# Reordering the first key/value groups of a fused linear-attention and gated-MLP kernel

## The chip, the core and the metric

The kernel runs on one core of a Trainium2 chip. The metric is device time in microseconds. Times come from several executions of each kernel (e5, e6, e9 and e10: one each); "before" is always run again on the same chip, and in the same rounds where there were several. Each profile is of one execution; its clock starts at the first instruction, so it ends about 1.7 us below the timed figure of that execution. The engines are named as in the profile: PE (matmul), PEld (weight load), DVE (vector), ACT (scalar), POOL, and SP, whose queue issues transfers.

## The reference, cut to what matters

```python
x = A_x                                         # 2048 tokens x 1024
h = x + linear_attention(layernorm(x), wqkv, wo)   # pk = phi(k); kv = sum_s pk^T v
h2 = h + reglu_mlp(layernorm(h), W_gate, W_up, W_down)
# phi(t) = (t + 1 if t > 0 else exp(t)) + 1e-6
```

The change touches only the start: layer norm of the first tokens, and the K and V projections.

## The kernel before

Tokens come in 16 blocks of 128. K and V are projected for two blocks at a time with a Strassen-like scheme: seven products P1 to P7 in place of eight, on sums of weight quarters (`w_sums`) and sums of token tiles (`x_sums`), both made on DVE. The groups run in the order k0, v2, k1, v3, k2, and so on: `k_group(p)` handles blocks 2p and 2p+1, `v_group(p)` runs two pairs ahead, and the first four blocks get their V directly (`v_piece`). Inside a group PE works through P1, P7, P6, P2, P5, P4, P3, and ACT copies partial results between PSUM banks, so that two later products can accumulate on the same start ("fork copies", fk1 after P1 and fk2 after P6):

```python
prod(a, X(0, 0), W(0, 0), True, "P1")
ident_act(bank(b), bank(a), ..., name + "fk1")     # P6 accumulates on this copy
hook(1)
prod(f, SX(2), TW(2), True, "P7")
ident_act(s7, bank(f), ...)
hook(2)
prod(b, SX(1), TW(1), False, "P6")
ident_act(bank(c), bank(b), ..., name + "fk2")     # P5 accumulates on this copy
hook(3)
prod(a, X(1, 0), W(1, 0), False, "P2")
...                                             # exp of this product
hook(4)
prod(c, SX(0), TW(0), False, "P5")
ident_act(sc, bank(c), ...)                     # P3 waits for this read
s22[0]()                                        # DVE add
hook(5)
prod(b, X(1, 1), TW(3), False, "P4");  s21[0]() # DVE add
hook(6)
...                                             # exp of the first sum
prod(c, SX(3), W(1, 1), False, "P3")
...                                             # exp of the second plain product (s12)
pend[1] = list(s22[2:]) + s12 + list(s21[1:])   # finished in the next group's hook(1)
```

A `hook` is where other work is put into the engines' queues: statistics of later blocks (on ACT, as squares in halves q0 and q1, or on DVE), norms and the transposes of the normalised blocks by DMA, and `kvacc`, 64 small matmuls for a pair of blocks that add pk^T v into one bank.

```python
def T1d(st):                                    # transpose by DMA, then the next load into that slot
    dma_t(sl_tx[k], xnT[:, :, st * P:(st + 1) * P], xn[:, k, :], ...)
    if st + NX1 < NST:
        load_x1(st + NX1)
```

Of the kernel before, what the change touches and what calls it, by code (L numbers as in the profile page):

```python
# [132 lines left out]
def bass_sequential_preLN__linear_attn_block__glu_gated_reglu__prompt_kernel(  # L133
# [28 lines left out]
    NST = S // P  # L162
# [5 lines left out]
    KH = NDC // 2  # L168
# [36 lines left out]
    with es:  # L205
# [44 lines left out]
        TWv = RW[:].bitcast(f16).rearrange("p (j k c) -> p j k c", j=4, k=KH)  # L250
# [156 lines left out]
        B_TWv = bufs("TWv_", 4)  # L407
# [484 lines left out]
        def ln1_stats_act(st, split=False):  # L892
            i = st % NX1
            k = len(ln1_a) % 3
            ln1_a[st] = k
            return act_stats(x1[:, i, :], B_x1[i], xn[:, st % NXN, :], B_xn[st % NXN], s1[:, k, :], B_s1[k],
                             "ln1_%d" % st, split)
# [60 lines left out]
                b = banks[i % len(banks)]  # L958
                mm(bank(b, 512), zeros_t[:, 0:P], zeros_t, True, True, [B_zeros], B_bank[b], "dummy")

        def v_piece(st, h, mid=()):
            b = alloc_bank(P1_POOL)
            nt = ND2 + h
            mid = dict(mid)
            for dc in range(NDC):
                if dc in mid:
                    mid[dc]()
                if st < 2:
                    xa, bx = xcT[:, st, dc, :], B_xcT[st][dc // HDC]
                else:  # L970
                    xa, bx = xnT[:, dc, st * P:(st + 1) * P], xnT_buf(st, dc)
                mm(bank(b, NW), xa, wkv[:, dc, nt * NW:(nt + 1) * NW],
                   dc == 0, dc == NDC - 1, [bx, B_wkv[nt][0 if dc < WKH else 1]], B_bank[b],
                   "v_%d_%d" % (st, h))
            v_copy(b, st, h)

        v_k = {}

# [7 lines left out]
        def v_copy(b, st, j):  # L986
            sc, rd = (1.0, []) if st >= 2 else (rstd[:, v_k[st], :], [B_rstd[v_k[st]]])
            PL.add("act", lambda e: e.activation(out=v_out(st, j), in_=gw(bank(b)), func=ACTF.Identity, scale=sc),
                   reads=[B_bank[b]] + rd, writes=[B_v[st % NV][j]], name="v_%d_%d" % (st, j))
# [45 lines left out]
        def sgroup(pool, tok_major, X, SX, W, TW, e11, e12, e21, e22, name, hooks=(), isphi=True, last=False):  # L1035

            hooks = dict(hooks)

            def prod(b, x, w, start, nm):
                (xf, xr), (wf, wr) = x, w  # L1040
                for kk in range(KH):
                    xa, wa = xf(kk), wf(kk)
                    l, r = (xa, wa) if tok_major else (wa, xa)
                    o = bank(b)
                    if len(r.shape) == 3:
                        o = o.rearrange("p (a b) -> p a b", b=r.shape[2])
                    mm(o, l, r, start and kk == 0, kk == KH - 1, xr + wr, B_bank[b], name + nm, skip=True)

            def hook(i):
                for f_ in pend.pop(i, ()):  # L1050
                    f_()
                if i in hooks:
                    hooks[i]()

            a = alloc_bank(pool)
            f = alloc_bank(pool)
            b = alloc_bank(pool, True)
            prod(a, X(0, 0), W(0, 0), True, "P1")
            ident_act(bank(b), bank(a), [B_bank[a]], [B_bank[b]], name + "fk1")
            hook(1)  # L1060
            prod(f, SX(2), TW(2), True, "P7")
            grp[0] += 1
            s7, b7 = [(atmp, B_at), (btmp[:, 1, :], B_bt[1])][grp[0] % 2]
            sc, bc = btmp[:, 0, :], B_bt[0]
            ident_act(s7, bank(f), [B_bank[f]], [b7], name + "s7")
            hook(2)
            c = alloc_bank(pool, True)
            prod(b, SX(1), TW(1), False, "P6")
            ident_act(bank(c), bank(b), [B_bank[b]], [B_bank[c]], name + "fk2")
            hook(3)  # L1070
            prod(a, X(1, 0), W(1, 0), False, "P2")
            for f_ in e11(bank(a), B_bank[a]):
                f_()
            hook(4)
            prod(c, SX(0), TW(0), False, "P5")
            ident_act(sc, bank(c), [B_bank[c]], [bc], name + "sc")
            s22 = e22(bank(f), B_bank[f], sc, bc)
            s22[0]()
            hook(5)
            prod(b, X(1, 1), TW(3), False, "P4")  # L1080
            s21 = e21(bank(b), B_bank[b], s7, b7)
            s21[0]()
            hook(6)
            for f_ in s22[1:2]:
                f_()
            prod(c, SX(3), W(1, 1), False, "P3")
            s12 = list(e12(bank(c), B_bank[c]))
            if isphi:
                s12.pop(0)()
            if last:  # L1090
                pend[1] = s12 + [s21[1]]
                return [s22[2], s21[2]]
            pend[1] = list(s22[2:]) + s12 + list(s21[1:])
            hook(7)

        pend = {}
# [42 lines left out]
        wv_ = wkv[:, :, D:2 * D]  # L1139
# [1004 lines left out]
            f_()  # L2144
        twk = w_sums(wkv, bw_k, tw_k, B_TWk, "TWk", KH)
        twv = w_sums(wv_, bw_v, tw_v, B_TWv, "TWv", KH)
        twq = w_sums(wq, bw_q, TWq, B_TWq, "TWq", KH // 2)

        v_piece(0, 0, {5: lambda: T1c(1, 0), 7: lambda: T1c(1, 1)})
# [13 lines left out]
        v_piece(2, 1, {4: lambda: T1(3), 6: m5})  # L2163
        q5()
        x_sums(0)
        twk.pop(0)()
        ln1_norm(4)
        T1d(4)
        m6, q6a, q6b = ln1_stats_act(6, True)
# [5 lines left out]
        twk.pop(0)()  # L2175
        twv.pop(0)()
        twv.pop(0)()
        v_piece(3, 1)
        for i in range(2):
            load_wq(i)  # L2180
        NP_ = NST // 2

        def kv_hooks(p, nq):

            sq = []
            A, B = 2 * p + 6, 2 * p + 7

            def k1():
                if p > 0 and A < NST:
                    ln1_stats(A)  # L2190
                for _ in range(nq[0]):
                    twq.pop(0)()

            def k4():
                if p == 0:
                    x_sums(2, 0)

            def k5():
                if p == 0:
                    x_sums(2, 1)  # L2200
                elif p + 2 < NP_:
                    x_sums(p + 2, 0)
                if p == 0:
                    m_, q0_, q_ = ln1_stats_act(B, True)
                    m_()
                    sq.extend([q0_, q_])
                while p > 0 and late_q:
                    late_q.pop(0)()

            def k6():  # L2210
                if p == 0:
                    twv.pop(0)()
                elif p + 2 < NP_:
                    x_sums(p + 2, 1)
            return {1: k1, 4: k4, 5: k5, 6: k6}, sq

        def norm(st):
            if st < NST:
                ln1_norm(st)
                T1d(st)  # L2220
# [5 lines left out]
        def kvaccs(p):  # L2226
            kvacc(2 * p)
            kvacc(2 * p + 1)

        late_q = []  # L2230
        NQ = {2: (0, 1), 3: (0, 1), 4: (0, 1), 5: (2, 2), 6: (1, 0)}
        for p in range(NP_):
            nq = NQ.get(p, (0, 0))
            hooks, sq = kv_hooks(p, nq)
            if p == 0:
                hooks[1], hooks[3] = q6a, q6b
            if p == NP_ - 1:
                hooks[7] = lambda: kvaccs(NP_ - 2)
            k_group(p, hooks)
            if p + 2 < NP_:  # L2240
                late = []

                def v3(p=p, sq=sq, late=late):
                    if sq:
                        sq.pop(0)()
                    if p == 0:
                        norm(6)
                        x_sums(1)
                    else:
                        norm(2 * p + 6)  # L2250
                        if 2 * p + 9 < NST:
                            m_, q0_, q_ = ln1_stats_act(2 * p + 9, True)
                            q0_()
                            late += [m_, q_]

                def v4(sq=sq):
                    if sq:
                        sq.pop(0)()

                def v5(p=p, late=late):  # L2260
                    norm(2 * p + 7)
                    if p == 0:
                        m_, q0_, q_ = ln1_stats_act(9, True)
                        m_()
                        late_q.extend([q0_, q_])
                    elif late:
                        late[0]()
                        late_q.append(late[1])

                def v6(p=p, nq=nq):  # L2270
                    kvaccs(p)
                    for _ in range(nq[1]):
                        twq.pop(0)()
                v_group(p + 2, {3: v3, 4: v4, 5: v5, 6: v6})
        assert not twq and not twv and not twk
        for i in range(ND2):
            load_wo(i)
# [1 line left out]
        for r in range(2):  # L2279
            for ct in range(NG // 2):  # L2280
                hooks = {}
# [41 lines left out]
        for p_ in range(NPASS):  # L2323
            fill = []
            for q in range(NPAIR):
                if q + 1 < NPAIR and p_ == 0:
                    fill = fill + t_sums((q + 1) * 2)
                mid = [[], [], [], [], []]
# [3 lines left out]
                if p_ == 0:  # L2332
# [4 lines left out]
                    if LQ <= q < LQ + TPP:  # L2337
                        m_, sq_, n_ = late_steps(q - LQ)
# [161 lines left out]
```

## Time and profile before

| | before |
|---|---|
| time, median (lowest to highest) of 4 runs | 719.93 us (719.61 to 719.95) |
| span of the profile | 718.3 us |
| PE / DVE / ACT busy | 99% / 83% / 53% |
| PE wait for the first fork copies of k0 and v2 | 1.6 us, the two of them |

PE is busy nearly all the time, and the profile's rows overlap (one of four matmuls is shown 1.03 us long, but the next starts 0.87 us later), so "busy" hides small gaps; gaps are read from the distance between the starts of products of the same form (0.87 us for four matmuls). The views that carry this are in the prediction.

### The profile page before, as it was taken

How to read it: one execution, taken by the hardware profiler on the slowest of the kernel's cores; microseconds unless marked ns; L12 is line 12 of the kernel's file. 1: busy time of each engine (PE TensorE's matmuls, PEld its weight loads, DVE VectorE, ACT ScalarE, POOL GpSimd, SP SyncE). 2: the span in 40 equal slices, each digit the busy share in tenths (PEclk: the TensorE clock that was granted, in tenths of full speed). 3: DMA queues.
4: the chain of work that ended last, by engine and by line, in shares of the span. 5: the costliest groups of instructions: out<-in, count | busy, mean ns of one | idle time of the engine just before them, and what ended most of it. 6: DMA issues, size and time to landing. Idle time of an engine off the chain costs nothing.

```text
span 718.3 us, 13075 instructions
## 1 busy us (share of the span) xinstructions
PE 711.7 (99%) x4979; PEld 387.4 (54%) x4979; DVE 597.4 (83%) x1009; ACT 383.9 (53%) x679; POOL 110.4 (15%) x178
## 2 busy tenths in 40 slices
PE   8999999999999999999999999999999999999998
PEld 4344444444444444444444568865555555547887
DVE  6988867799776889889888787878888888988885
ACT  4877656764941456686756102036766667643010
POOL 3321100000360103422320002320000000000331
PEclk9999999999999999999999999999999999999999
DMA  9852244014998787999998999995343534267996
GB/s 297 259 106 72 38 122 159 23 31 96 206 203 253 243 267 236 272 322 291 301 275 269 318 259 305 314 252 157 93 132 104 160 98 137 82 199 248 318 323 188
DMA packets 195102, 144.18 MB, mean 201 GB/s; under 512 B 53984, under 2 KB 172512, under 8 KB 195040
## 3 DMA queue, kind: packets, MB, share of 16 engines
q1 hardware_dynamic: 190048, 138.77, 66.2%
q0 software_dynamic: 4032, 3.67, 3.6%
q10 hardware_dynamic: 960, 0.92, 0.4%
q8 instruction: 39, 0.64, 0.4%
q14 instruction: 23, 0.19, 0.1%
HBM read 98.76 MB, written 32.51 MB: 183 GB/s over the span
## 4 chain that ended last, share of the span: by engine, by line
PE 93%; DVE 3%; DMA 2%; issue 1%; SPq 0%; ACT 0%; ACTq 0%
PE ps L777 93%; DMA RE<-in_A_x_dram 1%; DMA RAB<-in_A_wqkv_dram 1%; DVE RW L999 1%; DVE RC L999 1%; SPq L573 0%; DVE RWG L1024 0%; DVE RE L865 0%; DVE RX L1108 0%; DVE RE L1850 0%; DVE RX L862 0%; DVE st L791 0%; DVE RH L1024 0%; DVE RWG L1790 0%; ACT RX L858 0%
## 5 line engine op out<-in xcount | busy, mean ns | idle before, releaser
L782 ACT ACTIVATE ps<-ps 128x512 f32<-128x512 f32 (+1 forms) x233 | 122.3, 531 | 200.5 <-PE ps L777 171.8
L777 PE MATMUL ps<-RC,RO 128*128 128x512 f16 x616 | 143.0, 369 | 0.0
L777 PEld LDWEIGHTS ps<-RC,RO 128*128 128x128 f16 x616 | 60.3, 98 | 57.9
L777 PE MATMUL ps<-RH,RWG 128*128 128x512 bf16 (+1 forms) x396 | 91.2, 365 | 0.0
L777 PE MATMUL ps<-RC,RWG 128*128 128x512 f16 x320 | 79.0, 379 | 0.5 <-ACT ps L782 0.4
L782 ACT ACTIVATE RE<-ps 128x512 f32<-128x512 f32 (+3 forms) x85 | 49.3, 597 | 39.1 <-PE ps L777 28.9
L777 PE MATMUL ps<-RH,RO 128*128 128x512 bf16 (+1 forms) x256 | 63.3, 379 | 0.0
L777 PEld LDWEIGHTS ps<-RH,RWG 128*128 128x128 bf16 x396 | 38.7, 98 | 40.9 <-ACT ps L782 0.2
L1859 POOL DMA_DIRECT2D out_dram<-RX x20 | 18.0, 1282 | 260.9 <-DVE RX L1850 218.7
L777 PE MATMUL ps<-RW,RE 128*128 128x512 bf16 x256 | 57.6, 380 | 0.0
L777 PE MATMUL ps<-RW,RAB 128*128 128x256 f16 (+3 forms) x362 | 52.9, 301 | 0.0
L777 PEld LDWEIGHTS ps<-RC,RWG 128*128 128x128 bf16 (+1 forms) x320 | 30.0, 98 | 37.7 <-ACT ps L782 6.5
L777 PE MATMUL ps<-RAB 128*128 128x512 bf16 (+2 forms) x238 | 49.8, 348 | 0.0
L777 PEld LDWEIGHTS ps<-RW,RAB 128*128 128x128 f16 (+1 forms) x362 | 35.4, 98 | 14.4 <-DVE RX L1850 0.2
L1850 DVE TENSOR_TENSOR RE<-ps,RE 128x512 f32<-128x512 f32 x44 | 30.2, 687 | 15.1 <-PE ps L777 12.4
L1375 DVE TENSOR_TENSOR RO<-RWG 128x1024 f16<-128x1024 bf16 x54 | 36.9, 684 | 4.8 <-DMA RWG<-in_B_W_up_dram 4.8
L777 PEld LDWEIGHTS ps<-RW,RE 128*128 128x128 bf16 x256 | 23.9, 98 | 28.0 <-DVE RXH L1273 0.4
L777 PEld LDWEIGHTS ps<-RH,RO 128*128 128x128 f16 (+1 forms) x256 | 24.4, 98 | 27.2 <-ACT RX L782 1.5
L1623 DVE TENSOR_TENSOR RE<-ps,RE 128x512 f32<-128x512 f32 (+1 forms) x28 | 26.8, 958 | 14.1 <-PE ps L777 14.1
L1375 DVE TENSOR_TENSOR RO<-RWG,RO 128x1024 f16<-128x1024 bf16 x54 | 37.0, 685 | 0.5
L782 ACT ACTIVATE RAB<-ps 128x512 bf16<-128x512 f32 (+1 forms) x49 | 32.1, 654 | 5.6 <-PE ps L777 5.3
L862 DVE TENSOR_SCALAR RX<-RX 128x512 bf16<-128x512 bf16 x64 | 18.4, 288 | 19.5 <-ACT RX L858 18.6
(188 smaller groups left out, 1231.9 us busy)
## 6 DMA issues: line engine op xcount, KB each, us to landing
RWG<-in_B_W_gate_dram SPq DMA_DIRECT2D x28, 512.0 KB, 6.0
RWG<-in_B_W_up_dram SPq DMA_DIRECT2D x28, 512.0 KB, 5.1
RW<-l_scr SPq DMA_DIRECT2D x20, 448.0 KB, 6.1
RW<-in_B_W_down_dram SPq DMA_DIRECT2D x14, 512.0 KB, 5.1
t_scr<-RW SPq DMA_DIRECT2D x14, 512.0 KB, 4.8
l_scr<-RX SPq DMA_DIRECT2D x7, 1024.0 KB, 6.1
RE<-l_scr SPq DMA_DIRECT2D x15, 448.0 KB, 5.3
RE<-in_A_x_dram SPq DMA_DIRECT2D x23, 256.0 KB, 3.7
```

Source lines behind the costliest of these rows:

```text
L777: lambda e: e.matmul(out_ap, lhsT, rhs, start=start, stop=stop, skip_group_check=skip),
L782: PL.add("act", lambda e: e.activation(out=dst, in_=src, func=func), reads=reads, writes=writes, name=name)
L862: PL.add("dve", lambda e: e.tensor_scalar(out=Et[:, k, :], in0=Et[:, k, :], scalar1=1.0, scalar2=1e-6, op0=ALU.min, op1=ALU.add), reads=[] ...
L999: PL.add("dve", lambda e: e.tensor_tensor(out=t(j)(d), in0=in0(d), in1=in1(d), op=ALU.subtract), reads=reads, writes=[btw[j]], name="%s%d" ...
L1375: PL.add(eng, lambda e: e.tensor_tensor(out=tb(j, u), in0=f0(u), in1=f1(u), op=ALU.subtract), reads=[B_w[i + x] for x in r] + ([B_T[k + x] ...
L1623: PL.add("dve", lambda e: e.tensor_tensor(out=dst, in0=in0, in1=in1, op=op), reads=reads, writes=writes, name=name)
L1850: PL.add(eng, lambda e: e.tensor_tensor(out=dst, in0=in0, in1=in1, op=op), reads=reads, writes=writes, name=name)
L1859: PL.add("pool", lambda e: e.dma_start(dst, src, accum_op=ALU.add), reads=[bsrc], writes=[B_hscr[st]], slot=sl, name="acc_%d_%d" % (st, dh))
```

## The change

The intent is to shorten those waits: let the fork copies start earlier by moving other ACT work behind them, and give DVE less to do between the landing of the K weights and k0's end. The core of the diff:

```diff
+        twv[1:2] = w_sums(wv_, bw_v, tw_v, B_TWv, "TWv", KH // 2)[2:4]   # one V sum in two halves
         x_sums(0)
+        twv.pop(0)()                       # first half ahead of the K sums
         twk.pop(0)()
-        v_piece(3, 1)
+        b31 = v_piece(3, 1, copy=False)    # last direct V copy ...
-                hooks[1], hooks[3] = q6a, q6b
+                hooks[1], hooks[3] = lambda: v_copy(b31, 3, 1), q6a    # ... behind k0's fk1
-            pend[1] = list(s22[2:]) + s12 + list(s21[1:])
+            pend[1] = list(s22[2:]) + s12
+            if name in ("k0", "k1"):
+                pend[3] = list(s21[1:])    # last exp behind the next group's fk2
+            else:
+                pend[1] += list(s21[1:])
-                if p == 0:
-                    x_sums(2, 0)           # was at hook 4, ahead of the add
+                if p < 2:
+                    x_sums(p + 2)          # whole, at hook 5, behind the add
 # v2 (p == 0):
-  hook 3: q7 half, norm(6), x_sums(1)   hook 4: q7 half   hook 5: norm(7), stats(9)   hook 6: kvaccs(0)
+  hook 3: x_sums(1)   hook 5: q6b, both q7 halves, norm(6)   hook 7: kvaccs(0), norm(7), stats(9)
```

(The last two lines sum up a longer part of the diff; other cuts are renamings.)

More of the change, by code (lines that the diff above doesn't have):

```diff
@@ L959, in pe_dummies, with v_piece @@
                 mm(bank(b, 512), zeros_t[:, 0:P], zeros_t, True, True, [B_zeros], B_bank[b], "dummy")
-        def v_piece(st, h, mid=()):
+        def v_piece(st, h, mid=(), copy=True):
             b = alloc_bank(P1_POOL)
@@ L974, in v_piece @@
                    "v_%d_%d" % (st, h))
-            v_copy(b, st, h)
+            if copy:
+                v_copy(b, st, h)
+            return b
         v_k = {}
@@ L2192, in k1 @@
                     twq.pop(0)()
-            def k4():
-                if p == 0:
-                    x_sums(2, 0)
             def k5():
-                if p == 0:
-                    x_sums(2, 1)
+                if p < 2:
+                    x_sums(p + 2)
                 elif p + 2 < NP_:
@@ L2212, in k6 @@
                     twv.pop(0)()
-                elif p + 2 < NP_:
+                elif 1 < p < NP_ - 2:
                     x_sums(p + 2, 1)
-            return {1: k1, 4: k4, 5: k5, 6: k6}, sq
+            return {1: k1, 5: k5, 6: k6}, sq
         def norm(st):
@@ L2243, in v3, with v5, v6, v7 @@
                 def v3(p=p, sq=sq, late=late):
-                    if sq:
-                        sq.pop(0)()
                     if p == 0:
-                        norm(6)
-                        x_sums(1)
-                    else:
-                        norm(2 * p + 6)
-                        if 2 * p + 9 < NST:
-                            m_, q0_, q_ = ln1_stats_act(2 * p + 9, True)
-                            q0_()
-                            late += [m_, q_]
-                def v4(sq=sq):
-                    if sq:
-                        sq.pop(0)()
-                def v5(p=p, late=late):
-                    norm(2 * p + 7)
+                        x_sums(1)
+                        return
+                    norm(2 * p + 6)
+                    if 2 * p + 9 < NST:
+                        m_, q0_, q_ = ln1_stats_act(2 * p + 9, True)
+                        q0_()
+                        late += [m_, q_]
+                def v5(p=p, sq=sq, late=late):
+                    if p == 0:
+                        for f_ in [q6b] + sq:
+                            f_()
+                        norm(6)
+                        return
+                    norm(2 * p + 7)
+                    if late:
+                        late[0]()
+                        late_q.append(late[1])
+                def v6(p=p, nq=nq):
+                    if p > 0:
+                        kvaccs(p)
+                    for _ in range(nq[1]):
+                        twq.pop(0)()
+                def v7(p=p):
                     if p == 0:
+                        kvaccs(0)
+                        norm(7)
                         m_, q0_, q_ = ln1_stats_act(9, True)
@@ L2265, in v5 @@
                         late_q.extend([q0_, q_])
-                    elif late:
-                        late[0]()
-                        late_q.append(late[1])
-                def v6(p=p, nq=nq):
-                    kvaccs(p)
-                    for _ in range(nq[1]):
-                        twq.pop(0)()
-                v_group(p + 2, {3: v3, 4: v4, 5: v5, 6: v6})
+                v_group(p + 2, {3: v3, 5: v5, 6: v6, 7: v7})
         assert not twq and not twv and not twk
```

## The prediction

> **What bounds the kernel now.** I read the busy table and the chain that ended last first, then the chain in order of time, then the PE timeline and the waits of the first 60 us, where all edited code lies.
>
> ```profile
> PE 711.7 (99%) x4979; PEld 387.4 (54%) x4979; DVE 597.4 (83%) x1009; ACT 383.9 (53%) x679; POOL 110.4 (15%) x178
> PE 93%; DVE 3%; DMA 2%; issue 1%; SPq 0%; ACT 0%; ACTq 0%
> ...
> 15.70 5.84 DMA RAB<-in_A_wqkv_dram
> 21.54 0.02 issue
> 21.57 1.23 DVE RC L999
> ...
> 45.41 58.29 PE ps L777 x567
> ...
> 104.70 573.81 PE ps L777 x3807
> ```
>
> PE is the bound: from 45.4 us to the end the chain (start, length, what) is almost pure matmul. Before 45 us the chain runs through DVE: K-weight loads land at 21.54, then the weight sums (L999) start. So the only time on offer is PE's gaps in the first 45 us; if they shrink, everything after moves forward. Their size comes from the PE timeline (start, length, engine, line): groups of four 128x512 matmuls follow each other every 0.86 to 0.87 us (24.53, 25.39, 26.25), so any longer step is a gap.
>
> ```profile
> 23.10 1.03 PE L777 MATMUL ps<-RC,RWG 128*128 128x512 f16 x4
> 24.53 1.02 PE L777 MATMUL ps<-RC,RWG 128*128 128x512 f16 x4 [0.40 <-ACT ps L782]
> ...
> 29.70 1.03 PE L777 MATMUL ps<-RW,RWG 128*128 128x512 f16 x4
> 31.93 1.04 PE L777 MATMUL ps<-RW,RWG 128*128 128x512 f16 x4 [1.20 <-ACT ps L782]
> ...
> 34.65 1.03 PE L777 MATMUL ps<-RW,RAB 128*128 128x512 f16 x4
> 35.60 0.83 PE L777 MATMUL ps<-RE 128*32 128x33 bf16 x64
> 36.37 1.04 PE L777 MATMUL ps<-RAB,RH 128*128 128x512 bf16 x4
> ```
>
> Gaps: 23.10 to 24.53 is 1.43, or 0.57 too long (group k0, wait for its first fork copy, L782); 29.70 to 31.93 is 2.23, or 1.37 too long (group v2, same wait); 0.11 before v2's P5 (33.77); 0.09 before and 0.14 inside the small matmuls at 35.60, against 0.63 us for their repeat at 48.96. Together 2.3 us, 0.3% of the kernel. That is the ceiling of these two groups; the next group pair (k1, v3) has one 0.26 gap more, at 45.40.
>
> Whether ACT or what feeds ACT is to blame shows in the ACT and DVE timelines of that stretch:
>
> ```profile
> 23.17 1.22 DVE L999 TENSOR_TENSOR RC<-RAB,RC 128x2048 f16<-128x2048 bf16 x1
> ...
> 23.37 0.58 ACT L988 ACTIVATE RE<-ps 128x512 bf16<-128x512 f32 x1
> 23.84 0.59 ACT L782 ACTIVATE ps<-ps 128x512 f32<-128x512 f32 x1
> ...
> 29.55 0.69 DVE L1108 TENSOR_TENSOR RX<-ps,RX 128x512 f32<-128x512 f32 x1
> ...
> 30.27 0.63 ACT L858 ACTIVATE RX<-RX 128x512 bf16<-128x512 f32 x1 [1.32 <-DVE RX L1108]
> 30.80 0.58 ACT L858 ACTIVATE RX<-ps 128x512 bf16<-128x512 f32 x1
> 31.28 0.59 ACT L782 ACTIVATE ps<-ps 128x512 f32<-128x512 f32 x1
> ```
>
> The large gap is DVE's: ACT stood idle 1.32 us for the add at 29.55, then ran two exps and only then the fork copy.
>
> **What the skill says.** "TensorE: Matmul & The Clock Gate", section on the architectural detail, says ScalarE and VectorE are strict FIFO. The trace agrees: the fork copy at 31.28 starts right behind the two exps, though its own matmuls (28.84 to 29.87) were long done. "VectorE: DVE Perf Modes", the tier table, gives 1224 ns for a bf16 two-tensor operation on 2048 elements; the weight sums here take 1.22 us, and the half-size ones at L999 take 0.68. "Perfetto Trace Analysis", Optimizing Scalar/DVE Operations, advises breaking up instructions where they cause bubbles on another engine; the split of one weight sum is that.
>
> **The change, part by part.**
>
> 1. Half a V weight sum ahead of the K sums. DVE ends the x sums at 20.53 and idles until 21.57 for the K weights (1.03 us in its timeline). Half a sum (0.68) fits and costs nothing. Later one 1.22 us sum becomes 0.68: the K sums stay at 21.57, 23.17 and 24.76, because the landing fixes them; half V sum at 25.89, dependent sum at about 26.60 instead of 27.14, first phi step at 27.73 instead of 28.29. Gain 0.55 on DVE.
>
> 2. x sums of the next group whole behind the add. The one x sum (29.22, 0.33 us of issue distance) that stood ahead of the add goes behind it. Add at 27.73 + 0.93 = 28.66 instead of 29.55: 0.89 earlier. The sum itself then comes at 29.26, done 29.67; PE's P7 wants it at 29.70. It just fits.
>
> 3. Last direct V copy behind k0's fork copy. The fork copy can start when ACT is free, 23.37 instead of 23.84. But P6 of k0 also reads the third K sum, on DVE from 23.17 to 24.39 (first line of the fence above). With the 0.07 from a DVE end to a matmul start (29.63 to 29.70), P6 comes at 24.46 instead of 24.53: 0.07, not 0.47. The displaced half statistic (0.6) goes one place later, and its second half into v2, so the sc copy stays at about 27.3 and v2 starts at about 28.83 as before.
>
> 4. v2's first fork copy. Add 28.66, exp 0.72 later (before: 29.55 to 30.27) at 29.38, ACT being free of the statistic at 28.94; second exp 29.91, fork copy 30.39, P6 0.65 later at 31.04 against 31.93. Gain 0.89; 0.48 of the gap stays.
>
> 5. Last exp of a K group behind the second fork copy. Before, that exp (32.12, 0.5 of issue) stood ahead of s7 and the second fork copy. Now the latter only waits for P6: P5 comes 1.76 after P6 (two steps of 0.87), not 1.84. Another 0.08 to 0.11: P5 at 32.80 against 33.77.
>
> 6. Small KV matmuls behind P3. P4, P3 at 33.67 and 34.59, the 64 small ones at 35.46. They need the last phi; on DVE three phis of 0.93 from 32.58 end at 35.45. So no wait, and 0.63 instead of 0.77 plus 0.09. k1 starts at 36.1 instead of 37.24: 1.14 ahead.
>
> 7. The bill: ACT now has three half statistics and one full one after v2's sc copy (34.4 + 3 x 0.61, full one at 36.22, 1.06), so k1's fork copy comes at 37.28 and P6 at 37.94, where 37.82 was possible: 0.12 lost. Against 39.02 before, k1 is 1.08 ahead. In k1 to v3 ACT carries the same work as before (two half statistics, two exps, fork copy), so the 0.26 gap stays and the lead goes on unchanged.
>
> Sum: 0.07 + 0.82 + 0.1 + 0.2 - 0.1 = about 1.1 us. From 45 us PE has nothing but itself ahead of it, so 719.94 - 1.1 = **718.85 us**, 0.15% faster.
>
> **Rivals.** (a) **The transposed tiles of token block 7 become the wait.** Its norm is now queued behind v2 and behind POOL's statistics chain (before: 35.59 to 37.21, about 1.6 us after its last input). I put the norm at 38.7 instead of 38.57, while PE runs 1.1 ahead. The transpose of 39.13 took 3.3 us to land, others up to 4.3, and the x sums of v3 want it at about 42.5; they may wait 0.1 to 0.6. For it: all other work moves forward and this does not. Against: v3's P6 waits for ACT anyway until about 44.3, so most of it is hidden. If it bites: gain 0.5 to 0.8, 719.2 to 719.4. (b) **The K-weight landing at 21.54 and the K sums set everything**, and the ACT reordering is worth nothing. True for the k0 gap in my working, not for v2, where DVE itself gets shorter by 0.9. If v2's P6 were held by the x sums instead (SX2 done at about 30.5), no more than what I have is lost. (c) **The shift collides with weight DMA later**, or the backlog on DVE returns in the Q weight sums (89 to 104). The chain shows no DMA between 45 and the end, so at most tenths: 719.5. (d) **Better than I think**: if ACT has the k1 copy in time and v3's gap closes, 0.4 more: 718.4.
>
> **Range and chances.** The runs before span 0.34 us, as much as my uncertainty about single terms. (a) and (c) reach up to 719.6, (d) plus noise down to 718.2. The ceiling of 2.6 us (0.4%) excludes 2% faster; a loss of 14 us would need a new bound of the whole kernel, which nothing added here can make. So 718.2 to 719.6, within 2% almost surely.
>
> **What would show it.** Right if: the DVE idle time of 1.03 before 21.57 shrinks to about 0.35; k0's P6 moves by under 0.15; v2's P6 comes at about 31.0; the small matmuls come after P3 and k1 starts near 36.1; k1's P6 near 37.9 behind a late ACT copy; v3's P6 near 44.3; the long PE stretch after it has the old length. Wrong if k0's P6 comes at 24.1 (then the K sum did not hold it), if DVE waits for POOL or for the transposes at 38 to 43, or if the lead at 45 us is not there at the end.

## The result and the profile after

| | before | changed |
|---|---|---|
| median of 4 runs | 719.93 us | 719.42 us |
| lowest to highest | 719.61 to 719.95 | 719.03 to 719.63 |
| ratio of the fast runs (95% interval) | | 0.9993 (0.9976 to 1.0011) |
| span of the profile | 718.3 us | 717.7 us |

Ratios are the mean time of one kernel's fast runs over that of the other's of the same rounds, so not quite the ratio of the medians. All these runs were fast, that is, undisturbed, with a granted clock of 1.000. The change is worth 0.5 us, where 1.1 was forecast; the time is inside the range, and by the interval alone no difference would be shown. The traces, though, tell tenths: two profiles of the kernel before agree to 0.02 us up to v3 when counted from the same DVE instruction (e4 below).

The PE timeline of the changed kernel, at the places that were shown of before (start, length, engine, line, what; in brackets the idle time before and who ended it):

```profile
24.45 1.02 PE L777 MATMUL ps<-RC,RWG 128*128 128x512 f16 x4 [0.27 <-ACT RE L990]
...
30.97 1.04 PE L777 MATMUL ps<-RW,RWG 128*128 128x512 f16 x4 [0.27 <-ACT ps L782]
...
34.75 0.81 PE L777 MATMUL ps<-RAB,RH 128*128 128x512 bf16 x3
35.49 0.71 PE L777 MATMUL ps<-RE 128*32 128x33 bf16 x64
...
42.40 1.03 PE L777 MATMUL ps<-RAB 128*128 128x512 bf16 x4
44.19 1.91 PE L777 MATMUL ps<-RW,RWG 128*128 128x512 f16 x8 [0.76 <-DVE RWG L1026]
```

Up to 42 us everything is where it was forecast: k0's P6 at 24.45, v2's P6 at 30.97, the small matmuls at 35.49. Then v3's P7 comes 1.79 us after P1, not 0.87. In the kernel before, the same place looks like this:

```profile
43.42 1.03 PE L777 MATMUL ps<-RAB 128*128 128x512 bf16 x4
44.28 2.15 PE L777 MATMUL ps<-RW,RWG 128*128 128x512 f16 x8
46.27 1.03 PE L777 MATMUL ps<-RAB 128*128 128x512 bf16 x4
```

There P7 stood at 44.28: of a lead of one microsecond, 0.09 is left. The chain of the changed kernel (start, length, what) says who took it:

```profile
38.58 0.53 DVE RXH L903
39.11 0.88 DVE st L791 x2
39.99 3.69 DMA RAB<-RXH
43.68 0.02 issue
43.70 0.44 DVE RWG L1026
44.14 0.05 issue
44.19 5.13 PE ps L777 x84
```

A DMA that was not in the chain before: the transpose of token block 7 (RAB<-RXH). It was issued at 39.99 and landed at 43.68; the x sum of v3 on DVE (L1026) waited for it, and PE for that. The DVE timeline has the size of the wait:

```profile
43.70 0.76 DVE L1026 TENSOR_TENSOR RWG<-RAB 128x512 f16<-128x512 bf16 x2 [1.44 <-DMA RAB<-RXH]
```

The issue queue shows why it was issued so late. First the kernel before, then the changed one:

```profile
36.49 1.24 SPq L577 DMA_TRANSPOSE RAB<-RXH  x1
37.83 1.02 SPq L573 DMA_DIRECT2D RE<-in_A_x_dram  x1
39.13 1.23 SPq L577 DMA_TRANSPOSE RAB<-RXH  x1
```

```profile
38.08 1.23 SPq L577 DMA_TRANSPOSE RAB<-RXH  x1
39.42 0.53 SPq L573 DMA_DIRECT2D RE<-in_A_x_dram  x1
39.99 1.23 SPq L577 DMA_TRANSPOSE RAB<-RXH  x1
```

The norm of block 7 ended at 38.58 + 0.53 = 39.11 on DVE in both kernels (38.57 + 0.54 before), so it was not later by the clock, but it had not moved forward with PE either. But the change moved the norm of block 6 back to 37.53, so its transpose and the load behind it held the queue until 39.95, and block 7's transpose waited 0.9 us for the queue.

One thing more, far from the change: k6's first fork copy, with the same three waits in both programs. The kernel before, then the changed one (ACT timeline):

```profile
104.06 0.58 ACT L782 ACTIVATE ps<-ps 128x512 f32<-128x512 f32 x1 [3.02 <-PE ps L777]
```

```profile
103.47 0.58 ACT L782 ACTIVATE ps<-ps 128x512 f32<-128x512 f32 x1 [2.73 <-PE ps L777]
```

The idle time before it is 0.29 us shorter, and PE's lead rises there from 0.31 us (102.67 to 102.36) to 0.59 (105.57 to 104.98) and stays so: 0.57 at the end. About half of what the change gains in the trace comes from a place that it did not mean to touch.

### The profile page after: what moved, and what is told of

Read it like the earlier page. It is cut to its first block, busy times and chain, and to the rows that moved or that the text cites. A ratio compares the mean times of both kernels' runs of the same rounds, so it can differ in the third digit from the quotient of the medians.

```text
span 717.7 us, 13021 instructions
## 1 busy us (share of the span) xinstructions
PE 708.3 (99%) x4923; PEld 387.4 (54%) x4979; DVE 597.5 (83%) x1010; ACT 384.1 (54%) x679; POOL 109.1 (15%) x178
## 4 chain that ended last, share of the span: by engine, by line
PE 93%; DVE 3%; DMA 2%; issue 1%; SPq 1%; DVEq 0%
PE ps L777 93%; DMA RE<-in_A_x_dram 1%; DMA RAB<-in_A_wqkv_dram 1%; DVE RW L1001 1%; DMA RAB<-RXH 1%; DVE RC L1001 1%; SPq L573 1%; DVE RWG L1026 0%; DVE st L791 0%; DVE RE L865 0%; DVE RE L1856 0%; DVE RX L1114 0%; DVE RXH L903 0%; DVE RX L862 0%; DVE RWG L1796 0%
## 5 line engine op out<-in xcount | busy, mean ns | idle before, releaser
L777 PE MATMUL ps<-RH,RO 128*128 128x512 bf16 (+1 forms) x228 | 57.3, 380 | 1.5
L777 PEld LDWEIGHTS ps<-RAB 128*128 128x128 bf16 (+1 forms) x238 | 23.1, 98 | 20.3 <-ACT RAB L921 0.3
```

The costliest lines, as they stand in the source:

```text
L777: lambda e: e.matmul(out_ap, lhsT, rhs, start=start, stop=stop, skip_group_check=skip),
```

## The experiments

Total times of one kernel differ by up to 1.4 us between runs (before: 719.28 to 720.66). The profiles show much of why: the start of the first K sum on DVE, after the K weights' landing, lay anywhere from 20.58 to 21.82 us, and what follows moves with it. So the table gives places in microseconds **after the start of the first K sum** (all but the second column). They are worked out from the PE and DVE timelines and the last piece of the chain. "First K sum" means the first of the three that read the late K weights; one of the four K sums runs much earlier (at 15.99 before), so the "third K sum" of the prediction is the second of these.

| kernel | first K sum at | v2's P2 | k1's P7 | v3's P7 | v3's P2 | last DVE instruction | v3's P2 to there |
|---|---|---|---|---|---|---|---|
| before | 21.57 | 11.23 | 16.53 | 22.71 | 24.70 | 693.97 | 669.27 |
| e4, before again | 21.82 | 11.23 | 16.54 | 22.72 | 24.71 | 694.01 | 669.30 |
| changed | 21.48 | 10.37 | 15.52 | 22.71 | 24.45 | 693.49 | 669.04 |
| e1, block 6 early | 21.05 | 10.64 | 15.79 | 21.94 | 23.93 | 692.90 | 668.97 |
| e2, load late | 21.80 | 10.89 | 16.04 | 22.31 | 24.30 | 693.74 | 669.44 |
| e3, half sum alone | 21.02 | 10.73 | 16.04 | 22.23 | 24.22 | 693.50 | 669.28 |
| e5, before + one wait | 21.65 | 11.24 | 16.54 | 22.73 | 24.72 | 693.77 | 669.05 |
| e6, e1 + one wait | 21.22 | 10.36 | 15.51 | 21.66 | 23.65 | 692.91 | 669.26 |
| e7, no half sum | 20.58 | 11.43 | 16.58 | 23.76 | 25.51 | 694.50 | 668.99 |
| e8, all three | 21.23 | 10.23 | 15.39 | 21.54 | 23.26 | 692.36 | 669.10 |
| e9, small matmuls back | 21.33 | 10.36 | 15.99 | 22.71 | 24.46 | 693.46 | 669.00 |
| e10, x sum back | 20.97 | 10.80 | 15.95 | 22.78 | 24.53 | 693.49 | 668.96 |

Two things limit this table. In before, e4, e5 and changed the K weights landed 5.7 to 6.0 us after their issue and DVE waited for them; in the other eight traces they landed after 4.2 to 4.8 us, and DVE did not wait. With the half sum in place the first K sum then starts right behind it, up to 0.6 us after it could have, and counting from that sum leaves this cost out. And in e2 and e7 a POOL result held a norm between the K sums, so that the last K sum came 3.72 and 3.73 us after the first instead of 3.19: their rows count about 0.53 too much. With 0.53 taken off, e2 has v2's P2 at 10.36 and k1's P7 at 15.51, as the changed kernel does, v3's P2 at 23.77 and the end at 693.21.

My theory after the result: the lead is made as forecast and lost at v3's P7, because the norm of block 6 was moved behind v2 and its transfers then hold up block 7's transpose. Rivals: ACT or the x sums would have held v3 anyway; or the landing time of the transpose, not its issue, is what counts.

### e1: statistics and norm of block 6 back early

```diff
-  k0 hook 3: q6a            v2 hook 5: q6b, q7 halves, norm(6)
+  k0 hook 2: q6a, hook 3: q6b    v2 hook 3: norm(6), x_sums(1)    hook 5: q7 halves
```

> The changed kernel with the statistics and the norm of token block 6 put back early (first half statistic behind k0's third group of matmuls, second behind the next, norm ahead of the x sums in v2), all else as changed. Theory (the late norm of block 6 pushes the transpose of block 7 to 39.99 us through the shared issue queue, and v3's P7 waits for it): transpose of block 7 issued at about 39.1, landing at 42.4 to 42.8, v3's P7 at about 43.3 instead of 44.19, P6 at about 44.3 instead of 45.06; 0.7 us faster than the changed kernel, 718.7 us. Rival (the x sums or ACT would hold v3 anyway): P6 of v3 stays at 45.0 and the time at 719.4.

Measured: 718.83 us (718.43 to 719.16), before in the same rounds 720.09, ratio 0.9985 (0.9972 to 0.9997). The issue queue of this kernel:

```profile
35.71 1.23 SPq L577 DMA_TRANSPOSE RAB<-RXH  x1
37.04 0.52 SPq L573 DMA_DIRECT2D RE<-in_A_x_dram  x1
38.95 1.23 SPq L577 DMA_TRANSPOSE RAB<-RXH  x1
```

Block 7's transpose now follows its norm at once, and v3's P7 comes 0.87 after P1, without a gap:

```profile
42.12 1.03 PE L777 MATMUL ps<-RAB 128*128 128x512 bf16 x4
42.99 2.15 PE L777 MATMUL ps<-RW,RWG 128*128 128x512 f16 x8
```

The rival falls: neither ACT nor the x sums held P7. The end comes 0.59 us earlier than in the changed kernel, where 0.7 was forecast. A side effect showed in k0: the half statistic now stands in front of fk2 on ACT, and the step from P2 to P5 is 1.22 us in e1 and 1.16 in e6, the same order with one redundant wait, where the changed kernel has 0.90. In e1 fk1 was late as well, because the full statistic on ACT waited 0.38 us for a load of x: P6 came 3.27 after the first K sum instead of 2.96. e6 did not have this second delay and was 0.28 further ahead at v3's P2.

### e2: only the load of block 10 behind the transpose of block 7

```diff
     def T1d(st):
         dma_t(...)
+        if st == 6:
+            return
+        if st == 7:
+            load_x1(10)
         if st + NX1 < NST:
             load_x1(st + NX1)
```

> The changed kernel with only the load of x block 10 issued after the transpose of block 7 instead of before it. Theory (the queue that issues transposes and loads one after the other held the transpose of block 7 for 0.57 us): issue at 39.4 instead of 39.99, landing about 43.1, v3's P7 at 43.6, P6 at about 44.45; 0.5 us faster than the changed kernel, 718.9 us. Rival (the landing is set by traffic or by the time the transpose itself takes to finish behind the other one): issue earlier, landing still at 43.6 to 43.7, no gain.

Measured: 718.82 us median; four of five runs 718.39 to 718.97 and one, the profiled one, 720.02; ratio 0.9987 (0.9975 to 1.0000). That execution was late in the prologue (PE waited 1.7 us for weights there) and lost another 0.4 to 0.5 us between 213 and 228 us, where PE waited for another DMA (0.30 us of idle time shown, at 220.84); the times of the other runs leave no room for both. In its trace the issue queue has both transposes in a row, and v3's P7 comes 0.86 after P1 (43.25 to 44.11):

```profile
38.93 2.59 SPq L577 DMA_TRANSPOSE RAB<-RXH  x2
41.62 1.00 SPq L573 DMA_DIRECT2D RE<-in_A_x_dram  x2
```

Norm to landing fell from 4.57 us (39.11 to 43.68) to 3.07 at most (39.96 to 43.03, where the x sum started without a wait). Of these 1.5 us, 0.57 were the load's place in the queue. Most of the rest was landing time, 3.69 us in the changed kernel against at most 2.8 here. So both readings have a share: the load ahead of the transpose costs its issue, and a transpose issued right behind a load landed later. The second is seen in all twelve traces: from issue to landing block 7's transpose took 3.62 to 3.71 us in the six where the load was issued right ahead of it (at most 0.05 us between them: e4, changed, e5, e7, e9, e10), 3.31 and 3.45 where there were 0.29 and 0.78 us between (before, e3), and 2.72 to 2.98 in the other four. Why it lands later is not shown.

### e3: the half weight sum alone, on the kernel before

```diff
+        twv[1:2] = w_sums(wv_, bw_v, tw_v, B_TWv, "TWv", KH // 2)[2:4]
         x_sums(0)
+        twv.pop(0)()
```

> The kernel before with only the half V weight sum ahead of the K sums. Theory (DVE is what holds v2's first fork copy): add at 29.0 instead of 29.55, v2's P6 at 31.38 instead of 31.93, the norms of blocks 6 and 7 earlier as well, so no wait for the transposes in v3, and the lead of 0.55 us stays to the end: 719.4 us, as much as the whole change. Rival (ACT order is what counts): P6 moves by less than 0.2 and the time stays within 0.2 of before.

Measured: 719.32 us (719.01 to 719.80) against 720.09; ratio 0.9994 (0.9981 to 1.0008). In the trace v2's P2 is 0.50 earlier than before, v3's P2 0.48, the end 0.47: the lead is made and kept. One part of the change gives as much as the whole, 693.50 against 693.49 after the first K sum, and without the gain at k6, which e3 does not have (3.01 us of idle time there): at v3's P2 it is 0.23 ahead of the changed kernel. So on top of the half sum the four reorderings seem to lose a little (one trace of each). What the half sum fills varies with the weights' landing: DVE waited 1.03 and 1.16 us for them in the two profiles of before, but here they had landed (20.26) before it began. So 0.47 is its gain behind the first K sum, and what it is worth in the whole time when the weights are early is not shown; the interval leaves it open.

### e4: the kernel before, again

> The kernel before, unchanged, as a control: PE landmarks within 0.1 us of the first trace (v2's P6 31.93, v3's P6 45.40). Open: the first fork copy of the Q group at 104.06 came 0.36 us after its matmuls where the changed kernel has 0.25; if this is chance it differs here, and the end differs by up to 0.3 us.

Measured: 720.22 us median (719.58 to 720.43). The first K sum started 0.25 later than in the first profile, and the end came 0.29 later: nothing in between made it up. By the clock the expected 0.1 us was missed (v2's P6 at 32.18, not 31.93). Places after that sum agree to 0.02 up to v3 and to 0.04 at the end, so those numbers can be compared to some hundredths where the same thing bounds. The wait at k6's fork copy was again 3.02, so it is no chance.

### e5 and e6: one redundant wait on ACT

```diff
+            if e == "act" and n_ == 118:      # in group v7
+                eng.wait_ge(*again)           # an already satisfied wait, constant value
```

> The kernel before plus one redundant wait (already satisfied) on ACT in group v7, so that every later ACT instruction sits one place further. In both traces of the kernel before (and in e3) the first fork copy of k6, at about 104, started 0.28 us later after its matmuls than in the changed kernel, e1 and e2, although it waits for the same three things; its place among ACT's instructions is 187 in the first three kernels, 188 or 186 in the others. Theory (the place in the instruction stream makes the 0.28): the idle time before that copy falls from 3.02 to 2.73 us, and the stretch from v3's P2 to the last DVE instruction from 669.27 to 669.0 us. Rival (the changed order of work before makes it): it stays at 3.02 and 669.27.

> The same redundant wait in e1's kernel, which moves that fork copy of k6 from place 186 to 187. Theory: the idle time before it rises from 2.73 to 3.02 us and P2 of k6 comes 0.28 later against v3's P2; the stretch from v3's P2 to the last DVE instruction goes from 668.97 to about 669.25 us. Rival: both stay.

The ACT timelines, e5 then e6, at k6's first fork copy:

```profile
103.91 0.58 ACT L786 ACTIVATE ps<-ps 128x512 f32<-128x512 f32 x1 [2.73 <-PE ps L781]
```

```profile
102.66 0.58 ACT L786 ACTIVATE ps<-ps 128x512 f32<-128x512 f32 x1 [3.01 <-PE ps L781]
```

Both ways as the theory said: a useless wait made the kernel before 0.22 us shorter from v3's P2 on (669.05 against 669.27) and e1's kernel 0.29 longer (669.26 against 668.97). The 0.28 us belongs to the instruction's place in ACT's stream (187 slow; 186 and 188 not, as counted for e5's forecast), not to the work moved. All twelve traces fit: 3.01 to 3.02 us in before, e4, e3 and e6, 2.73 in the other eight. Why that place is slow is not settled. The Trainium skill's "Runtime: NRT & Kernel Launch", Instruction fetch mechanics, says instructions stream in blocks of 256 and that crossing a block is mostly hidden; a block border near that place is one possible reason, but no view shows one. Each of the two was profiled and timed once: 719.91 and 718.62 us, before 719.64 on the same chip.

### e7: the change without the half sum

```diff
-        twv[1:2] = w_sums(...)[2:4]
         x_sums(0)
-        twv.pop(0)()
```

> The changed kernel with the half V weight sum undone, all its other parts kept. Theory (in the changed kernel the transpose of block 7 sets v3, and it comes from the DVE chain, so DVE time is worth its full size): v2's P6 at about 31.5, transpose of block 7 issued 0.55 later, v3's P7 at about 44.7; 0.5 us slower than the changed kernel, 719.9 us, no better than before: the four reorderings together are then worth nothing. Measured from the first K sum to the last DVE instruction: 694.0 against 693.49. Rival (the reorderings carry the gain): 719.4 to 719.5.

Measured: 719.55 us (719.47 to 719.86), before 719.64; ratio 0.9998 (0.9985 to 1.0012). The times decide nothing here: the median is nearer to the rival's 719.4 to 719.5 than to the forecast 719.9, and the interval takes in both. In the trace the K weights had landed before DVE was free (at 20.58), and a POOL result held a norm by 0.46, so "after the first K sum" is not comparable as it stands. Counted from the last K sum (24.31 in e7, 24.76 before) the last DVE instruction comes after 690.77 us, before after 690.78, changed after 690.29: the reorderings without the half sum gain nothing at the end, though e7 has the shorter wait at k6. That is one trace of each. It also shows DVE waiting 1.42 us for the transpose of block 7 again.

### e9 and e10: two other parts put back

```diff
 # e9:  v2 hook 6: kvaccs(0) again, not hook 7
 # e10: k0 hook 4: x_sums(2, 0); hook 5: x_sums(2, 1)
```

> The changed kernel with only the small KV matmuls of the first pair put back ahead of v2's P3. Theory (v3's P7 waits for the transpose of block 7, whose chain runs over DVE and the issue queue, so PE's lead before it is lost whatever its size): the small matmuls wait for the last phi and k1 starts about 0.5 us later than in the changed kernel (its P7 at 16.0 instead of 15.52 after the first K sum), but v3's P7 stays at about 22.7 and the end at 693.5 after the first K sum. Rival (this part carries part of the gain): the end comes 0.3 to 0.5 later.

> The changed kernel with only one thing put back: the first x sum of v2 ahead of the add of k0. Theory: v2's P6 0.33 later (9.8 instead of 9.49 after the first K sum), v3's P7 unchanged at about 22.7, the end unchanged at about 693.5, because the order within DVE does not change when DVE reaches the norm of block 7. Rival: the 0.33 us stays to the end.

Measured (one run each): 719.27 and 718.95, before 719.44. The traces decide. In e9 k1's P7 came at 15.99 instead of 15.52, in e10 v2's P2 at 10.80 instead of 10.37: both parts do what they were meant to. But v3's P7 stayed at 22.71 and 22.78, and the end at 693.46 and 693.49 against 693.49. In the change as it stands these two parts are worth nothing, because their gain ends in the wait for the transpose.

### e8: a version that beats both

e1 and e2 together, and in k0 and k1 the exp of the second plain product behind the next fork copy:

```diff
-            if isphi:
+            if isphi and name not in ("k0", "k1"):
                 s12.pop(0)()
```

> A version meant to beat both: the changed kernel with e1's early statistics of block 6, e2's late load, and in k0 and k1 the exp of the second plain product behind the next group's first fork copy instead of ahead of it. Theory (what is left are ACT's 0.43 before v2's P6 and 0.26 before v3's P6): from the first K sum to v2's P6 9.2 us instead of 9.49 (changed) and 10.36 (before), to v3's P2 about 23.3 instead of 24.45, to the last DVE instruction about 692.3 instead of 693.49 (changed) and 693.97 (before); 718.3 us. Rival (DVE's phis, ending about 14.1 us after the first K sum, now hold the small KV matmuls and take the lead back): no better than e1, 692.9 and 718.8.

Measured: 718.07 us (717.69 to 718.25), before 719.64 in the same rounds, ratio 0.9976 (0.9962 to 0.9989). After the first K sum it ends at 692.36, forecast 692.3: 1.6 us ahead of before (0.28 of it at k6, where e8 has the shorter wait), 1.1 of the changed kernel. Its PE timeline through v3:

```profile
41.90 1.03 PE L777 MATMUL ps<-RAB 128*128 128x512 bf16 x4
42.77 1.89 PE L777 MATMUL ps<-RW,RWG 128*128 128x512 f16 x8
44.49 1.03 PE L777 MATMUL ps<-RAB 128*128 128x512 bf16 x4
```

P1 to P2 of v3 is 2.59 us, three steps of 0.86; it was 3.53 in the changed kernel (42.40 to 45.93). The rival (the phis would hold the small matmuls) falls. What e2's part adds to e1's order was not tested alone; in e1 the load was already 1.4 us ahead of block 7's transpose.

## Why the prediction was right or wrong

The time lay in the range, and steps 1 to 7 hold to a tenth up to k1, but the sum was twice the measured gain. By its own steps:

- **Step 1, half sum: right.** Second half at 25.81 (forecast 25.89), first phi step at 27.67 (27.73). e3 shows it carries 0.47 to the end alone, counted after the first K sum.
- **Step 2, x sums behind the add: right** in its place (add at 28.60, forecast 28.66), and e10 shows 0.43 at v2's P2 for it. But none of it reaches the end.
- **Step 3, last V copy: right.** The fork copy moved to 23.36, P6 only from 24.53 to 24.45: the third K sum held it (23.08 + 1.22 = 24.30, and P6 0.15 later, where 0.07 was assumed). The profile names the V copy (L990) as releaser, but in e6 P6 started at 24.18, 0.15 after the same K sum and before that copy ended (24.57). Rival (b) is true of k0, and of k0 only.
- **Steps 4 and 5: right.** Fork copy 30.33 (30.39), P6 30.97 (31.04), P5 32.74 (32.80).
- **Step 6: right** (P3 at 34.59 was forecast, the small matmuls at 35.46; they came at 35.49). e9 shows it gains 0.47 by k1, and nothing at the end.
- **Step 7 failed.** Its first half held: k1's fork copy at 37.38 (37.28). The failing sentence is the last: "so the 0.26 gap stays and the lead goes on unchanged". v3 was limited by something else than ACT, and the lead fell from 1.0 to 0.25 at v3's P2. This was rival (a), named but given too little: I put the norm of block 7 at 38.7 (it was 38.58), took its transpose as issued right after it, and overlooked that block 6's transpose (1.23) and load (0.53) now sat directly ahead in the same queue. That delayed the issue by 0.9, to 39.99. I also took the wait for hidden behind ACT; but P7, which comes ahead of P6 on PE, needs the sum that waited, and P6 needs two further sums on DVE, the last of which ended at 44.93. P6 came at about 45.06 (P2 less one step of 0.87), where ACT alone would have allowed 44.4, fork copy at 43.74 plus 0.65. So two of the prediction's own signs of being wrong were there: DVE waited 1.44 us for that transpose, 42.26 to 43.70, and v3's P6 was not near 44.3.
- **A term that was not in the sum:** 0.28 us at k6, from the place of one instruction (e5, e6). The prediction called the chain from 45 us on almost pure matmul and passed over this place in it (103.71 to 104.70). Without it the changed kernel would have gained only about 0.25 us. So two errors, of about -0.75 and +0.25, went into the forecast of 1.1, and that the time came near rival (a)'s 719.4 and inside the range is in part luck.
- **Rival (c)** did not occur: outside k6 the lead stays within 0.03 us from v3's P2 to the end. **Rival (d)** did not occur in the change, but e8 shows that what it names was there.
- The places of the Trainium skill that the prediction names agree with the later traces too: in e8 the fork copy put ahead of an exp on ACT ran ahead of it (29.93, the exp at 30.43), the full weight sums took 1.22 to 1.23 us again, and splitting one of them was the part that paid.

## What to carry to other kernels

When work on the critical engine moves forward, list everything that does not move with it, and follow each transfer to its issue queue: a transfer is only as early as the ones ahead of it in that queue. Moving "unimportant" work back can put two transfers next to each other and make the second one the new bound. And before crediting a gain of some tenths to a reordering, compare step by step where in the trace it arises; here half of it was an accident of instruction placement.

## What the Trainium skill lacked or had wrong

- "Runtime: NRT & Kernel Launch", Instruction fetch mechanics, calls the cost of crossing an instruction block mostly hidden. Whether this is that crossing is open, but an instruction's place alone cost 0.28 to 0.29 us here, exposed on PE, at a copy behind three waits (e5: 3.02 to 2.73 us of idle; e6: 2.73 to 3.01).
- "DMA: Bandwidth & Descriptors", DMA Transpose (X-bar), gives constraints but no issue time or landing time for a 128x1024 transpose between SBUF tiles on trn2 (another section of the page counts sequencer cycles per transpose of earlier generations, but none for this size). Between 20 and 95 us these traces show mostly 1.23 to 1.33 us on the issuing queue per transpose (at most 2.44), mostly 0.52 to 0.59 per load of x of 256 KB (at most 1.77), and 2.7 to 4.6 us from issue to landing (the first transpose of all: 7.6 to 8.5).
- No page I looked at says what a load ahead in the same queue does to a transpose's landing: 3.62 to 3.71 us with the load right ahead, 2.72 to 2.98 with none within 1.3 us (block 7, e2 above).
- No page I looked at says how far the landing of the first loads varies: the load that the first K sum needs landed 4.2 to 4.8 us after its issue in eight profiles and 5.7 to 6.0 in four, and totals of the kernel before spread by up to 1.4 us.
